# Two small loads of x and two of w1 in order of need, and tile 0's first matmuls ahead of tile 1's transposes, in a dense layer with Mish

## The chip, the cores and the metric

The kernel runs on one core of a Trainium2 chip. The metric is the device time of one execution in microseconds (us), as the median of several executions. The core has a tensor engine (PE, which multiplies matrices and transposes), a vector engine (DVE), a scalar engine (ACT, which applies functions such as Mish), GpSimd (POOL) and SyncE (SP, used here to issue transfers). Transfers run on DMA engines that SP and ACT give work to, each through a queue of its own.

## The reference

x is 2048 x 512, w1 is 512 x 1792, b1 has 1792 numbers, w2 is 1792 x 512, all bf16. The output is `mish(x @ w1 + b1) @ w2`:

```python
def reference(x, w1, b1, w2):
    h = jnp.einsum("bsd,df->bsf", x, w1) + b1
    sp = jnp.log1p(jnp.exp(-jnp.abs(h))) + jnp.where(h > 0, h, jnp.zeros_like(h))
    act = h * jnp.tanh(sp)
    return jnp.einsum("bsf,fd->bsd", act, w2)
```

## The kernel before, in words

Everything is cut into tiles of 128. The 2048 rows of x are 16 row tiles in four blocks of four. The inner size 512 has four steps k, and the hidden size 1792 has 14 tiles f. A first matmul (line 165) takes a 128 x 128 piece of w1 (k, f) as weights and streams x, transposed, past it; four of them, one for each k, add up in one PSUM bank of 512 columns. ACT reads the bank, adds the bias and writes Mish of it to `a_sb` (line 171). The second matmul (line 198) adds up 14 products of `a_sb` and w2 for each row tile; DVE copies the sum to `o_sb` (line 186) and SP stores it (line 190).

x has to be transposed. For row tiles 2 to 15 the transfer itself does that (`load_xT`, line 102). Row tiles 0 and 1 are loaded as they are into `x_nat` (line 112), one load of 256 KB in which a partition gets two neighbouring rows; PE transposes them against an identity matrix that POOL builds (`transpose_x`, line 141) and DVE copies the result from PSUM to `xT` (line 150). The output rows of tiles 0 and 1 are stored through the same pairing of rows (`out01`, line 189).

The order on each engine is written out by hand. A wait stops an engine's own queue, so what stands behind it waits as well.

- SP issues, in this order: x of tiles 0 and 1; w1 of f 0-3, k 2-3; w1 of f 4-7, k 0-1 and k 2-3; xT of tiles 2-3; w1 of f 8-13 in two; w2 in two; xT of the other blocks; later the stores.
- ACT waits for a memset of DVE (line 108), issues w1 of f 0-3, k 0-1 (line 117) and then b1 (line 118), and loads its function table (line 128).
- PE runs ten dummy matmuls on constants (line 134; five of 512 columns and five of 128, the list `WARM`), then eight transposes in three groups: k 0, k 1, and k 2-3, both row tiles in each. Then come the first matmuls of f 0-3, k by k, on the 256 columns of row tiles 0 and 1; the same for f 4-7; then f 0-7 on the 256 columns of row tiles 2 and 3, and behind each f its Mish. From f 8 on, all matmuls have 512 columns.
- DVE copies the three groups of transposes, then waits for b1 and brings it into one column for each f (lines 209 to 214), then copies outputs.

`pe.wait` in `mm1_step` (lines 161 to 164) makes a matmul wait for its bank, its piece of w1, and its columns of `xT`.

Of the kernel before, what the change touches and what calls it, by code (L numbers as in the profile page):

```python
# [4 lines left out]

P = 128
WARM = (512,) * 5 + (128,) * 5
GROUPS = ((0, 4), (4, 8), (8, 14))
BLOCKS = (512, 512, 512, 512)
LAST = 96  # L10

# [22 lines left out]
def bass_standalone__dense_activation_mish__prompt_kernel(  # L34
# [10 lines left out]
    BF, F32 = dt.bfloat16, dt.float32  # L45
# [3 lines left out]
    KT, FT = D // P, F // P  # L49
    assert (S, D, F) == (2048, 512, 1792) and sum(BLOCKS) == S  # L50
    x2, out2 = x[0], out[0]
# [3 lines left out]
    F0 = 8  # L55

    with ExitStack() as es:
        def sb(name, shape, t):
            return es.enter_context(nc.sbuf_tensor(name, shape, t))

        x_nat = sb("x_nat", [P, 2, D], BF)
        xT = sb("xT", [P, KT, S], BF)
        w1_sb = sb("w1_sb", [P, KT, F], BF)
        w2_sb = sb("w2_sb", [P, FT, D], BF)
        b1_nat = sb("b1_nat", [FT, P], BF)
# [4 lines left out]
        ident = sb("ident", [P, P], BF)  # L70
        a_sb = sb("a_sb", [P, FT, S], BF)
        o_sb = sb("o_sb", [P, S // P, D], BF)
        ps = es.enter_context(nc.psum_tensor("ps", [P, 8, 512], F32))

        def sem(name):
            return es.enter_context(nc.semaphore(name))

        sp = Stream(nc.sync, None)
        pe = Stream(nc.tensor, sem("c_pe"))
        dve = Stream(nc.vector, sem("c_dve"))  # L80
        act = Stream(nc.scalar, sem("c_act"))
        pool = Stream(nc.gpsimd, sem("c_pool"))

        def load(q, dst, src, name, transpose=False):
            s = sem(name)
            (q.eng.dma_start_transpose if transpose else q.eng.dma_start)(dst, src).then_inc(s, 16)
            return (s, 16)

        t_w1, t_w2, t_xT = {}, {}, {}

        def load_w1(q, ks, a, b):
            t = load(q, w1_sb[:, ks, a * P:b * P], w1v[:, ks, a * P:b * P], "s_w1_%d_%d" % (ks.start, a))
            for f in range(a, b):
                for k in range(ks.start, ks.stop):
                    t_w1[k, f] = t

        def load_w2(a, b):
            t = load(sp, w2_sb[:, a:b, :], w2v[:, a:b, :], "s_w2_%d" % a)
            for f in range(a, b):
                t_w2[f] = t  # L100

        def load_xT(lo, hi):
            t = load(sp, xT[:, :, lo:hi], x2[lo:hi, :], "s_xT%d" % lo, True)
            for j in range(lo // P, hi // P):
                t_xT[j] = t

        t_bz = dve.mark(nc.vector.memset(b1_pad[:, :], 0.0))  # L107
        act.wait(t_bz)

        x01 = x2[0:2 * P, :].rearrange("(p j) d -> p j d", j=2)  # L110
        out01 = out2[0:2 * P, :].rearrange("(p j) d -> p j d", j=2)
        t_xn = load(sp, x_nat[:, :, :], x01, "s_xn")
        for a, b in GROUPS:
            if a == F0:
                load_xT(2 * P, 4 * P)
            for ks in (slice(0, 2), slice(2, KT)):
                load_w1(act if (a, ks.start) == (0, 0) else sp, ks, a, b)
        t_b1 = load(act, b1_nat[:, :], b1.rearrange("(j p) -> j p", p=P), "s_b1")
        load_w2(0, 5)
        load_w2(5, FT)  # L120
        for s in range(1, len(BLOCKS)):
# [4 lines left out]
        t_id = pool.mark(pool.eng.affine_select(ident[:, :], ones[:, :], pattern=[[1, P]], compare_op=ALU.is_equal,  # L126
                                                fill=0.0, base=0, channel_multiplier=-1))
        act.eng.preload_act_table(ACT.Mish)  # L128

        c_w = nc.const_aps.tensor(1.0, [P, P], BF)  # L130
        c_m = nc.const_aps.tensor(1.0, [P, 512], BF)

        def dummy(n):
            nc.tensor.matmul(ps[:, 7, 0:n], c_w, c_m[:, 0:n], start=True, stop=True)  # L134

        free = [[] for _ in range(8)]
        t_cp = {}
        t_mish = {}


        def transpose_x(bank, ks):
            pe.wait(t_xn, t_id, *free[bank])
            psb = ps[:, bank, :].bitcast(BF)
            for i, k in enumerate(ks):
                for j in range(2):
                    mm = nc.tensor.transpose(psb[:, (2 * i + j) * P:(2 * i + j + 1) * P],  # L146
                                             x_nat[:, j, k * P:(k + 1) * P], ident[:, :])
            n = len(ks)
            dve.wait(pe.mark(mm))
            t = dve.mark(nc.vector.tensor_copy(xT[:, ks[0]:ks[0] + n, 0:2 * P],  # L150
                                               psb[:, 0:2 * n * P].rearrange("p (k t) -> p k t", k=n)))
            for k in ks:
                t_cp[k] = t
            free[bank] = [t]

        def mm1_step(s, f, k, bank, j0=0, j1=None):
            j1 = BLOCKS[s] // P if j1 is None else j1
            lo, hi = j0 * P, j1 * P
            first = k == 0 and j0 == 0
            if first:  # L160
                pe.wait(*free[bank])
            pe.wait(t_w1[k, f])
            for j in range(starts[s] // P + j0, starts[s] // P + j1):
                pe.wait(t_cp[k] if j < 2 else t_xT[j])
            return nc.tensor.matmul(ps[:, bank, lo:hi], w1_sb[:, k, f * P:(f + 1) * P],  # L165
                                    xT[:, k, starts[s] + lo:starts[s] + hi], start=first,
                                    stop=(k == KT - 1 and hi == BLOCKS[s]))
# [8 lines left out]
        s_out = sem("s_out")  # L176
        n_out = 0

        def put(i, lo, hi, bank, t_mm, q):
            nonlocal n_out  # L180
            if q is act:
                act.wait(t_mm)
                t = act.mark(act.eng.activation(o_sb[:, i, lo:hi], ps[:, bank, 0:hi - lo], ACT.Copy))  # L183
            else:
                dve.wait(t_mm)
                t = dve.mark(nc.vector.tensor_copy(o_sb[:, i, lo:hi], ps[:, bank, 0:hi - lo]))  # L186
            free[bank] = [t]
            q.wait(t)
            dst = out01[:, i, lo:hi] if i < 2 else out2[i * P:(i + 1) * P, lo:hi]
            q.eng.dma_start(dst, o_sb[:, i, lo:hi]).then_inc(s_out, 16)  # L190
            n_out += 1

        def mm2(i, lo, hi, bank, q=sp):
            s = max(b for b in range(len(BLOCKS)) if starts[b] <= i * P)
            pe.wait(*free[bank])
            for f in range(FT):
                pe.wait(t_w2[f], t_mish[s, f])
                mm = nc.tensor.matmul(ps[:, bank, 0:hi - lo], a_sb[:, f, i * P:(i + 1) * P], w2_sb[:, f, lo:hi],  # L198
                                      start=(f == 0), stop=(f == FT - 1))
            put(i, lo, hi, bank, pe.mark(mm), q)  # L200


        for n in WARM:
            dummy(n)
        transpose_x(6, (0,))
        transpose_x(5, (1,))
        transpose_x(4, (2, 3))
        dve.wait(t_b1, t_bz)
        t_b1p = dve.mark(nc.vector.tensor_copy(b1_pad[0:FT, :], b1_nat[:, :]))  # L209
        dve.wait(t_b1p)  # L210
# [1 line left out]
            t_b1t = dve.mark(nc.vector.transpose(b1_t[c * 32:(c + 1) * 32, :], b1_pad[:, c * 32:(c + 1) * 32]))  # L212
        dve.wait(t_b1t)
        t_b1c = dve.mark(nc.vector.tensor_copy(b1_sb[:, :], b1_t[:, 0:FT]))  # L214
        for a, b in GROUPS[:2]:
            for k in range(KT):
                for f in range(a, b):
                    mm1_step(0, f, k, f, 0, 2)
        for f in range(F0):
            for k in range(KT):  # L220
                mm = mm1_step(0, f, k, f, 2, 4)
            mish(0, f, f, pe.mark(mm))

        for s in range(len(BLOCKS)):
            for f in range(F0 if s == 0 else 0, FT):
                bank = f % 8 if s == 0 else 4 + f % 4
                for k in range(KT):
                    mm = mm1_step(s, f, k, bank)
                mish(s, f, bank, pe.mark(mm))
            for i in range(starts[s] // P, starts[s + 1] // P):  # L230
                if i < S // P - 1:
                    mm2(i, 0, D, i % 4)
                else:
                    mm2(i, 0, D - LAST, i % 4)
                    mm2(i, D - LAST, D, (i + 1) % 4, act)
# [29 lines left out]
```

## Time and profile before

| What | us |
|---|---|
| three runs | 105.36, 105.79, 104.87 |
| their median | 105.36 |
| the profiled execution, its own time | 105.59 |
| its span, from the first to the last instruction | 104.3 |
| PE busy | 101.6 |
| ACT busy | 38.9 |
| DVE busy | 13.2 |

The profile follows one execution. Each engine's instructions have a start and a length; PEld is the loading of weights on PE, which runs beside its matmuls. Matmuls overlap in their pipeline, so the length of one is longer than the step from one to the next. A queue row (SPq, ACTq) shows when an engine issued a transfer and how long issuing took; the rows of transfers give the time from issue to landing. Times in the rows are counted from the start of the span.

### The profile page before, as it was taken

How to read it: one execution, taken by the hardware profiler on the slowest of the kernel's cores; microseconds unless marked ns; L12 is line 12 of the kernel's file. 1: busy time of each engine (PE TensorE's matmuls, PEld its weight loads, DVE VectorE, ACT ScalarE, POOL GpSimd, SP SyncE). 2: the span in 40 equal slices, each digit the busy share in tenths (PEclk: the TensorE clock that was granted, in tenths of full speed). 3: DMA queues.
4: the chain of work that ended last, by engine and by line, in shares of the span. 5: the costliest groups of instructions: out<-in, count | busy, mean ns of one | idle time of the engine just before them, and what ended most of it. 6: DMA issues, size and time to landing. Idle time of an engine off the chain costs nothing.

```text
span 104.3 us, 1168 instructions
## 1 busy us (share of the span) xinstructions
PE 101.6 (97%) x512; PEld 50.0 (48%) x512; DVE 13.2 (13%) x26; ACT 38.9 (37%) x58; POOL 0.7 (1%) x6
## 2 busy tenths in 40 slices
PE   6999999999999999999999999999999999999992
PEld 2689744444444444444444444444444444444452
DVE  0340000022220000022220000022112000021222
ACT  1303998000027777200007777500005777700000
POOL 2000000000000000000000000000000000000000
PEclk9999999999999999999999999999999999999999
DMA  2999999981101000010111000001111000001111
GB/s 48 360 296 356 351 257 142 258 202 50 37 14 50 0 0 6 0 49 1 50 50 50 0 0 0 9 0 50 50 50 50 0 0 0 0 6 50 50 50 50
DMA packets 13377, 7.94 MB, mean 76 GB/s; under 512 B 7868, under 2 KB 13244, under 8 KB 13372
## 3 DMA queue, kind: packets, MB, share of 16 engines
q1 hardware_dynamic: 12928, 7.58, 27.6%
q10 hardware_dynamic: 444, 0.29, 0.9%
q8 instruction: 4, 0.07, 0.3%
q14 instruction: 1, 0.01, 0.0%
HBM read 3.94 MB, written 2.10 MB: 58 GB/s over the span
## 4 chain that ended last, share of the span: by engine, by line
PE 97%; ACT 0%; issue 0%
PE ps L165 47%; PE ps L198 46%; PE ps L134 3%; PE ps L146 1%; ACT o_sb L183 0%
## 5 line engine op out<-in xcount | busy, mean ns | idle before, releaser
L171 ACT ACTIVATE a_sb<-ps,b_sb 128x512 bf16<-128x512 f32 x56 | 37.4, 693 | 50.1 <-PE ps L165 50.1
L165 PE MATMUL ps<-xT,w_sb 128*128 128x512 bf16 (+1 forms) x256 | 50.0, 357 | 0.0
L198 PE MATMUL ps<-w_sb,a_sb 128*128 128x512 bf16 (+2 forms) x238 | 49.0, 366 | 0.0
L165 PEld LDWEIGHTS ps<-xT,w_sb 128*128 128x128 bf16 x256 | 25.4, 100 | 23.6
L198 PEld LDWEIGHTS ps<-w_sb,a_sb 128*128 128x128 bf16 x238 | 22.6, 98 | 26.1
L186 DVE CAST o_sb<-ps 128x512 bf16<-128x512 f32 (+1 forms) x16 | 11.0, 685 | 84.8 <-PE ps L198 84.8
L183 ACT ACTIVATE o_sb<-ps 128x96 bf16<-128x96 f32 x1 | 0.3, 251 | 11.4 <-PE ps L198 11.4
L134 PE MATMUL ps<-const-bfloat16-1.0 128*128 128x512 bf16 (+1 forms) x10 | 2.8, 469 | 0.8 <-PEq L250 0.8
L134 PEld LDWEIGHTS ps<-const-bfloat16-1.0 128*128 128x128 bf16 x10 | 1.2, 142 | 2.2 <-issue 2.2
L128 ACT ACT_TABLE_LOAD x1 | 1.3, 1283 | 2.2 <-issue 2.2
L150 DVE COPY xT<-ps 128x256 bf16<-128x256 bf16 (+1 forms) x3 | 0.9, 336 | 3.2 <-PE ps L146 3.1
L146 PE MATMUL ps<-ident,x_nat 128*128 128x128 bf16 x8 | 1.0, 311 | 0.0
L146 PEld LDWEIGHTS ps<-ident,x_nat 128*128 128x128 bf16 x8 | 0.8, 142 | 0.3 <-DMA x_nat<-in_x_dram 0.3
L212 DVE STREAM_TRANSPOSE b_t<-b_pad 32x32 bf16<-32x32 bf16 x4 | 0.8, 202 | 0.1
L126 POOL TENSOR_SCALAR_AFFINE_SELECT ident<-ones 128x128 bf16<-128x128 bf16 x1 | 0.3, 294 | 0.1
L107 DVE MEMSET b_pad<- 32x64 uint32 x1 | 0.1, 112 | 0.9 <-PEq L250 0.9
L124 POOL MEMSET ones<- 128x128 bf16 x1 | 0.2, 205 | 0.3 <-POOLq L250 0.3
L209 DVE COPY b_pad<-b_nat 14x128 bf16<-14x128 bf16 x1 | 0.2, 182 | 0.2 <-DMA b_nat<-in_b_dram 0.2
L214 DVE CAST b_sb<-b_t 128x14 f32<-128x14 bf16 x1 | 0.2, 175 | 0.0
L250 POOL MEMSET const-bfloat16-1.0<- 128x1 bf16 x1 | 0.1, 102 | 0.0
L250 POOL MEMSET const-uint8-127<- 128x1 uint8 x1 | 0.1, 102 | 0.0
L250 POOL MEMSET const-float32-0.0<- 128x1 f32 x1 | 0.1, 99 | 0.3 <-issue 0.3
(1 smaller groups left out, 0.1 us busy)
## 6 DMA issues: line engine op xcount, KB each, us to landing
out_dram<-o_sb SPq DMA_DIRECT2D x15, 128.0 KB, 1.7
w_sb<-in_w_dram SPq DMA_DIRECT2D x1, 1152.0 KB, 10.1
w_sb<-in_w_dram SPq DMA_DIRECT2D x3, 256.0 KB, 4.2
w_sb<-in_w_dram SPq DMA_DIRECT2D x2, 384.0 KB, 5.4
w_sb<-in_w_dram SPq DMA_DIRECT2D x1, 640.0 KB, 7.2
x_nat<-in_x_dram SPq DMA_DIRECT2D x1, 256.0 KB, 2.8
w_sb<-in_w_dram ACTq DMA_DIRECT2D x1, 256.0 KB, 3.4
out_dram<-o_sb SPq DMA_DIRECT2D x1, 104.0 KB, 1.7
```

The source lines that it names most:

```text
L126: t_id = pool.mark(pool.eng.affine_select(ident[:, :], ones[:, :], pattern=[[1, P]], compare_op=ALU.is_equal, fill=0.0, base=0, channel_mu ...
L128: act.eng.preload_act_table(ACT.Mish)
L134: nc.tensor.matmul(ps[:, 7, 0:n], c_w, c_m[:, 0:n], start=True, stop=True)
L146: mm = nc.tensor.transpose(psb[:, (2 * i + j) * P:(2 * i + j + 1) * P], x_nat[:, j, k * P:(k + 1) * P], ident[:, :])
L150: t = dve.mark(nc.vector.tensor_copy(xT[:, ks[0]:ks[0] + n, 0:2 * P], psb[:, 0:2 * n * P].rearrange("p (k t) -> p k t", k=n)))
L165: return nc.tensor.matmul(ps[:, bank, lo:hi], w1_sb[:, k, f * P:(f + 1) * P], xT[:, k, starts[s] + lo:starts[s] + hi], start=first, stop=( ...
L171: t = act.mark(act.eng.activation(a_sb[:, f, starts[s]:starts[s + 1]], ps[:, bank, 0:BLOCKS[s]], ACT.Mish, bias=b1_sb[:, f:f + 1]))
L183: t = act.mark(act.eng.activation(o_sb[:, i, lo:hi], ps[:, bank, 0:hi - lo], ACT.Copy))
L186: t = dve.mark(nc.vector.tensor_copy(o_sb[:, i, lo:hi], ps[:, bank, 0:hi - lo]))
L198: mm = nc.tensor.matmul(ps[:, bank, 0:hi - lo], a_sb[:, f, i * P:(i + 1) * P], w2_sb[:, f, lo:hi], start=(f == 0), stop=(f == FT - 1))
L212: t_b1t = dve.mark(nc.vector.transpose(b1_t[c * 32:(c + 1) * 32, :], b1_pad[:, c * 32:(c + 1) * 32]))
L250: nc = _bacc.Bacc("TRN2", target_bir_lowering=False, num_devices=1)
```

## The change

- `WARM` loses its five dummies of 128 columns; a list `GAP` with one dummy of 128 is run behind the transposes of row tile 0.
- x of tiles 0 and 1 is loaded in two loads of 128 KB, one for each row tile, without the pairing of rows; the stores of these tiles follow that.
- SP issues, in this order: x tile 0; w1 of f 0-3, k 0; x tile 1; w1 of f 0-3, k 1; w1 of f 0-3, k 2-3; w1 of f 4-7 in two; xT of tiles 2-3; w1 of f 8-13 in two; then as before. ACT issues none of w1.
- ACT no longer waits for DVE's memset. It loads its table, waits for x tile 0, and then issues b1.
- `transpose_x` now works on one row tile. PE transposes tile 0 (k 0, then k 1-3), runs the dummy, multiplies tile 0 by k 0 of f 0-3 (128 columns), transposes tile 1 (k 0-1, then k 2-3), multiplies tile 0 by k 1, then tile 1 by k 0 and k 1. From k 2 of f 0-3 on, both row tiles are taken together as before.

```diff
-WARM = (512,) * 5 + (128,) * 5
-GROUPS = ((0, 4), (4, 8), (8, 14))
+WARM = (512,) * 5
+GAP = (128,)
...
-        act.wait(t_bz)
-
-        x01 = x2[0:2 * P, :].rearrange("(p j) d -> p j d", j=2)
-        out01 = out2[0:2 * P, :].rearrange("(p j) d -> p j d", j=2)
-        t_xn = load(sp, x_nat[:, :, :], x01, "s_xn")
-        for a, b in GROUPS:
-            if a == F0:
-                load_xT(2 * P, 4 * P)
-            for ks in (slice(0, 2), slice(2, KT)):
-                load_w1(act if (a, ks.start) == (0, 0) else sp, ks, a, b)
-        t_b1 = load(act, b1_nat[:, :], b1.rearrange("(j p) -> j p", p=P), "s_b1")
+        def load_x(j):
+            t_xn[j] = load(sp, x_nat[:, j, :], x2[j * P:(j + 1) * P, :], "s_xn%d" % j)
+
+        load_x(0)
+        load_w1(sp, slice(0, 1), 0, 4)
+        load_x(1)
+        load_w1(sp, slice(1, 2), 0, 4)
+        load_w1(sp, slice(2, KT), 0, 4)
+        for ks in (slice(0, 2), slice(2, KT)):
+            load_w1(sp, ks, 4, F0)
+        load_xT(2 * P, 4 * P)
+        for ks in (slice(0, 2), slice(2, KT)):
+            load_w1(sp, ks, F0, FT)
         load_w2(0, 5)
...
         act.eng.preload_act_table(ACT.Mish)
+        act.wait(t_xn[0])
+        t_b1 = load(act, b1_nat[:, :], b1.rearrange("(j p) -> j p", p=P), "s_b1")
...
-        def transpose_x(bank, ks):
-            pe.wait(t_xn, t_id, *free[bank])
-            psb = ps[:, bank, :].bitcast(BF)
+        def transpose_x(j, bank, ks):
+            pe.wait(t_xn[j], t_id, *free[bank])
+            psb = ps[:, bank, 0:2 * P].bitcast(BF)
             for i, k in enumerate(ks):
-                for j in range(2):
-                    mm = nc.tensor.transpose(psb[:, (2 * i + j) * P:(2 * i + j + 1) * P],
-                                             x_nat[:, j, k * P:(k + 1) * P], ident[:, :])
+                mm = nc.tensor.transpose(psb[:, i * P:(i + 1) * P], x_nat[:, j, k * P:(k + 1) * P], ident[:, :])
...
-        transpose_x(6, (0,))
-        transpose_x(5, (1,))
-        transpose_x(4, (2, 3))
+        transpose_x(0, 6, (0,))
+        transpose_x(0, 5, (1, 2, 3))
+        for n in GAP:
+            dummy(n)
+        for k in range(2):
+            for f in range(4):
+                mm1_step(0, f, k, f, 0, 1)
+            if k == 0:
+                transpose_x(1, 6, (0, 1))
+                transpose_x(1, 4, (2, 3))
         dve.wait(t_b1, t_bz)
...
-        for a, b in GROUPS[:2]:
-            for k in range(KT):
-                for f in range(a, b):
+        for k in range(2):
+            for f in range(4):
+                mm1_step(0, f, k, f, 1, 2)
+        for a in (0, 4):
+            for k in range(0 if a else 2, KT):
+                for f in range(a, a + 4):
                     mm1_step(0, f, k, f, 0, 2)
```

More of the change, by code (lines that the diff above doesn't have):

```diff
@@ L87, in load @@
             return (s, 16)
-        t_w1, t_w2, t_xT = {}, {}, {}
+        t_xn, t_w1, t_w2, t_xT = [None] * 2, {}, {}, {}
         def load_w1(q, ks, a, b):
@@ L138, in bass_standalone__dense_activation_mish__prompt_kernel @@
         t_mish = {}
-        def transpose_x(bank, ks):
-            pe.wait(t_xn, t_id, *free[bank])
-            psb = ps[:, bank, :].bitcast(BF)
+        def transpose_x(j, bank, ks):
+            pe.wait(t_xn[j], t_id, *free[bank])
+            psb = ps[:, bank, 0:2 * P].bitcast(BF)
             for i, k in enumerate(ks):
-                for j in range(2):
-                    mm = nc.tensor.transpose(psb[:, (2 * i + j) * P:(2 * i + j + 1) * P],
-                                             x_nat[:, j, k * P:(k + 1) * P], ident[:, :])
+                mm = nc.tensor.transpose(psb[:, i * P:(i + 1) * P], x_nat[:, j, k * P:(k + 1) * P], ident[:, :])
             n = len(ks)
             dve.wait(pe.mark(mm))
-            t = dve.mark(nc.vector.tensor_copy(xT[:, ks[0]:ks[0] + n, 0:2 * P],
-                                               psb[:, 0:2 * n * P].rearrange("p (k t) -> p k t", k=n)))
+            t = dve.mark(nc.vector.tensor_copy(xT[:, ks[0]:ks[0] + n, j * P:(j + 1) * P],
+                                               psb[:, 0:n * P].rearrange("p (k t) -> p k t", k=n)))
             for k in ks:
-                t_cp[k] = t
+                t_cp[j, k] = t
             free[bank] = [t]
@@ L163, in mm1_step @@
             for j in range(starts[s] // P + j0, starts[s] // P + j1):
-                pe.wait(t_cp[k] if j < 2 else t_xT[j])
+                pe.wait(t_cp[j, k] if j < 2 else t_xT[j])
             return nc.tensor.matmul(ps[:, bank, lo:hi], w1_sb[:, k, f * P:(f + 1) * P],
@@ L188, in put @@
             q.wait(t)
-            dst = out01[:, i, lo:hi] if i < 2 else out2[i * P:(i + 1) * P, lo:hi]
-            q.eng.dma_start(dst, o_sb[:, i, lo:hi]).then_inc(s_out, 16)
+            q.eng.dma_start(out2[i * P:(i + 1) * P, lo:hi], o_sb[:, i, lo:hi]).then_inc(s_out, 16)
             n_out += 1
```

## The prediction

> **What bounds the kernel now.** I read the page first: the span, the engines' shares, and the chain of work that ended last.
>
> ```profile
> span 104.3 us, 1168 instructions
> ...
> PE 101.6 (97%) x512; PEld 50.0 (48%) x512; DVE 13.2 (13%) x26; ACT 38.9 (37%) x58; POOL 0.7 (1%) x6
> ...
> PE 97%; ACT 0%; issue 0%
> ```
>
> TensorE (PE) is busy 97% of the span and carries 97% of the chain. Then I read the same chain in order of time (start us, length us, what).
>
> ```profile
> 0.84 2.83 PE ps L134 x10
> 3.67 1.03 PE ps L146 x8
> 4.70 13.06 PE ps L165 x88
> 17.75 12.09 PE ps L198 x56
> 29.84 12.09 PE ps L165 x56
> ```
>
> From 3.67 on, PE goes from transposes to matmuls without a pause that the chain shows. A full-width matmul costs 12.09 / 56 = 0.216 us, and one of 256 columns half of it, 0.108. Is PE as quick at the start? Two stretches of equal length, line 165 alone (busy us, matmuls that touch the stretch, then clock, DMA share, GB/s):
>
> ```profile
> 4.53:6.40 1.87, 1.87 (x9) 1.00 1.15 337
> 6.40:8.27 1.87, 1.87 (x20) 1.00 1.12 297
> ```
>
> The shape is the same (256 columns, f tiles 0-7), but nine touch the first stretch and twenty the second. Nine in 1.87 is 0.208 each, twice 0.108. The granted-clock column says 1.00 in both rows, so it hides this; the counts show PE at half rate until about 6.40. **Everything the diff moves on PE lies in this slow stretch, so 1 us saved there brings only 0.5 us at the end**, unless the turn at 6.40 moves as well. That is the question of this case.
>
> The weight loads say what PE waits for at the start, and the same pair of rows prices small dummies.
>
> ```profile
> 2.50 0.15 PEld L134 LDWEIGHTS ps<-const-bfloat16-1.0 128*128 128x128 bf16 x1 [0.28 <-issue]
> 2.93 0.47 PEld L134 LDWEIGHTS ps<-const-bfloat16-1.0 128*128 128x128 bf16 x4 [0.28 <-issue]
> 3.66 0.77 PEld L146 LDWEIGHTS ps<-ident,x_nat 128*128 128x128 bf16 x8 [0.26 <-DMA x_nat<-in_x_dram]
> ```
>
> A 512-column dummy holds PE 2.93 - 2.50 = 0.43 us. Four 128-column loads in 0.47 are three steps of 0.107 and one load of 0.15; so a 128-column step is 0.107 us here. PE then stands 0.26 us until x has landed, and the first transpose starts at 3.66.
>
> **The loads.** The queue rows, then issue to landing of the first ones (KB, us):
>
> ```profile
> 0.81 0.39 SPq L86 DMA_DIRECT2D x_nat<-in_x_dram  x1
> 1.26 1.44 SPq L86 DMA_DIRECT2D w_sb<-in_w_dram  x3
> 2.74 1.30 SPq L86 DMA_TRANSPOSE xT<-in_x_dram  x1
> ```
>
> ```profile
> x_nat<-in_x_dram SPq DMA_DIRECT2D x1, 256.0 KB, 2.8
> w_sb<-in_w_dram ACTq DMA_DIRECT2D x1, 256.0 KB, 3.4
> ```
>
> ```profile
> w_sb<-in_w_dram SPq DMA_DIRECT2D x1, 256.0 KB, 3.9
> ```
>
> ```profile
> xT<-in_x_dram SPq DMA_TRANSPOSE x1, 5.0
> ```
>
> ScalarE's queue and its part of the start:
>
> ```profile
> 1.02 0.43 ACTq L86 DMA_DIRECT2D w_sb<-in_w_dram  x1
> 1.47 0.72 ACTq L86 DMA_DIRECT2D b_nat<-in_b_dram  x1
> 2.22 1.28 ACT L128 ACT_TABLE_LOAD   x1 [2.22 <-issue]
> 9.62 3.00 ACT L171 ACTIVATE a_sb<-ps,b_sb 128x512 bf16<-128x512 f32 x5 [6.12 <-PE ps L165]
> ```
>
> So x lands at 0.81 + 2.8 = 3.6, w1 k 0-1 of f 0-3 at 1.02 + 3.4 = 4.4, k 2-3 at 1.26 + 3.9 = 5.2, xT of tiles 2-3 at 2.74 + 5.0 = 7.7. One 256 KB load follows another by 0.74 to 0.8 us: in order, at full DMA. How fast the bytes come in (last column GB/s):
>
> ```profile
> 1.80:2.40 0.60, 0.60 (x3) 0.15 (x1) 0.00 (x0) 0.18 (x1) 0.00 (x0) 1.00 0.99 126
> 2.40:2.90 0.50, 0.50 (x2) 0.15 (x1) 0.00 (x0) 0.50 (x1) 0.00 (x0) 1.00 0.85 301
> 2.93:3.66 0.73, 0.73 (x6) 0.47 (x5) 0.00 (x0) 0.58 (x1) 0.00 (x0) 1.00 1.03 356
> ```
>
> **Part 1: x in two loads, w1 k 0 and k 1 between and behind.** Tile 0 is 128 KB (131 kB) where 256 KB stood. At those rates 76 kB are in by 2.40 and 131 kB by 2.58; the whole 262 kB were in by 3.00. The gain lies between 0 (the landing is latency, not bytes) and 0.42. I take 0.30, nearer the upper end, since later landings follow the bytes. So x tile 0 lands at 3.31 and its first transpose starts at 3.36. After it each 128 KB costs 0.37, half of 0.74: w1 k 0 at 3.68, x tile 1 at 4.05, k 1 at 4.42, k 2-3 at 5.2, the same bytes as now by the same time. SP issues all of it, one per 0.48 (1.44 / 3): the five issues start at 0.81, 1.26, 1.74, 2.22, 2.70, and with 2.5 from issue to landing no load can beat 4.24 (x tile 1), 4.72 (k 1) and 5.20 (k 2-3). I use these later values.
>
> **Part 2: the order on PE.** DVE's rows give the way from a transpose to a matmul.
>
> ```profile
> 4.09 1.06 DVE L150 COPY xT<-ps 128x256 bf16<-128x256 bf16 x3 [3.11 <-PE ps L146]
> 5.33 0.18 DVE L209 COPY b_pad<-b_nat 14x128 bf16<-14x128 bf16 x1 [0.17 <-DMA b_nat<-in_b_dram]
> 5.54 0.90 DVE L212 STREAM_TRANSPOSE b_t<-b_pad 32x32 bf16<-32x32 bf16 x4
> 6.48 0.17 DVE L214 CAST b_sb<-b_t 128x14 f32<-128x14 bf16 x1
> ```
>
> ```profile
> L150 DVE COPY xT<-ps 128x256 bf16<-128x256 bf16 x2 | 0.5, 292 | 3.1 <-PE ps L146 3.1
> L150 DVE COPY xT<-ps 128x512 bf16<-128x512 bf16 x1 | 0.4, 423 | 0.1
> ```
>
> Two transposes from 3.66 release the copy at 4.09, 0.43 later; one does so after 0.32. A copy of 128 columns isn't in the trace. The line through 292 ns (256) and 423 ns (512) gives 227 for 128 and 161 for none, so it lies between 0.16 and 0.29; I take 0.23. From a copy's end (4.09 + 0.29 = 4.38) to the first matmul (4.53) are at most 0.15, part of it the weights' wait; I take 0.13. All in slow-stretch time:
>
> - 3.36 first transpose of tile 0; four and the GAP dummy, 5 x 0.107, end at 3.90.
> - Copy of k 0: 3.36 + 0.32 = 3.68 to 3.91; first matmul at 4.04. **A stall of 0.14 that is not there now.** w1 k 0 (3.68, or 1.26 + 2.5 = 3.76) is not what it waits for.
> - Four matmuls of 128 columns to 4.47; tile 1's four transposes (x landed 4.24) to 4.90; k 1 of tile 0 (weights 4.72; its copy of three blocks is done by about 4.5) to 5.32.
> - Tile 1's copy of k 0-1: 4.47 + 0.43 + 0.29 + 0.13 = 5.32: just in time. Eight matmuls of 128 to 6.18.
>
> Sixteen matmuls of 128 columns are eight of 256. The kernel before does its eight from 4.53 in 8 x 0.208, to 6.20. So the sum at that point is -0.30 (x sooner) + 0.107 (GAP) + 0.14 (stall) + 0.03 (handing over, rounding) = **-0.02 us, worth -0.01 us at the end.** The five small dummies cost nothing either way: they stand in the wait for x, which lasts from 2.93 to 3.36 without them; an x before 2.93 would be needed for them to matter. With the bounds (gain 0 to 0.42, copy 0.07 faster to 0.06 slower) the sum is -0.21 to +0.34, worth -0.11 to +0.17.
>
> **Part 3: later loads.** xT of tiles 2-3 is issued eighth on SP rather than fifth, at about 4.2 (0.81 + 7 x 0.48) instead of 2.74. The bytes ahead of it are the same 1280 KB, so by bytes it lands at 7.7 again; with its own 5.0 from issue it would be 9.2. PE needs it after 32 matmuls: 9 to 6.40 and 23 x 0.108 give 8.9. I take 7.8, free, since most of the 5.0 was queueing behind loads that are now gone before it is issued; at 9.2 it costs 0.3 at full rate. w1 of f 8-13 and w2 keep their place in bytes behind it.
>
> b1 is issued by ScalarE once x tile 0 is in, 3.31 rather than 1.47. From its issue to DVE's use were 5.33 - 1.47 = 3.86; then the chain to 6.65, 1.32. That gives 8.5; the first Mish starts at 9.62, released by PE. Cover 1.1; and DVE holds no transpose copy behind that wait. The table load moves to about 1 on ScalarE, which has nothing before 9.62. Output rows of tiles 0 and 1 change place in DRAM, not size: nothing, as the end comes from later tiles.
>
> **The rivals.** *PE's turn to full rate comes later (slower).* Today PE starts at 0.84, stands 0.26 once, and turns at 6.40, 5.56 after its start. The changed kernel stands from 2.93 (2.50 + 0.43) to 3.36 and again 0.14: 0.57, twice as much and earlier. If the standing makes the clock's count begin anew at 3.36, the turn comes at 8.92, 2.52 late, at half rate **+1.26: 106.6**. It decides once the standing is too much; that 0.26 was not is all the trace says. The Trainium skill ("TensorE: Matmul & The Clock Gate", Part 1) gives free-running windows of about 3.4 us, of which one must be busy; by it a missed window would cost an estimated 1.7 us rather than 1.26. Its Part 4 says of transposes that they don't count as busy in the same way; by that rule the 0.85 us of transposes would add to both kernels' standing, making this rival likelier. The trace has one turn and can't show either. Against it: eight transposes and a wait stood ahead of the turn now too. Chance 0.18.
>
> *The change doesn't do what it says*: tile 0 lands with tile 1, as the queue's start is what takes the time (the 126 GB/s row). Then PE starts at 3.66 as now, and the GAP and the stall remain: +0.28 slow, +0.14; with xT late (+0.3) **105.6 to 105.8**. Chance 0.14.
>
> *The gain comes whole and more*: x tile 0 at 3.1 or below (0.5 sooner), w1 k 0 right behind, no second stall: -0.5 + 0.25 slow, **105.2**. For: the last quarter of the load came at 301 to 356 GB/s. Chance 0.13. *The turn comes sooner*, by 2 us or more, for a reason not in the rows (other executions differ by 0.9 us): **104.3**, chance 0.05.
>
> **How the numbers follow.** The profiled execution took 105.59, with 104.3 span; the median of the runs is 105.36, 0.23 lower, and they reach from 104.87 to 105.79. 105.59 - 0.01 - 0.23 is 105.35; I say 105.3. Chances: forecast (within 0.2 of now) 0.50, rivals as above. Low end: the early case and the runs' spread, 104.8; high end: up to the late turn, 106.5, leaving half of that rival out. About 1% (1.05 us) is what a measurement of this kernel can tell from no change. Faster by over 1% is the sooner turn: 0.05. Slower by over 1% is the late turn, whose 1.26 the spread may hide: 0.17. Same: 0.78.
>
> **What would show it.** First transposes between 3.2 and 3.5 (x split right); a gap of about 0.14 ahead of the first matmul, released by DVE's copy (the stall); 128-column steps of 0.107; two half-length stretches around 6.40 with about nine and twenty matmuls' worth of columns (turn unmoved); no PE wait at about 8.9 (xT in time). It is wrong if the half-rate stretch ends at 8 or later, if PE waits for x tile 1 or w1 by more than 0.2, or if Mish waits for the bias.

## The result

The changed kernel takes 105.94 us (median of 19 executions, 105.64 to 107.56) against 105.27 for the kernel before (19 executions, 104.66 to 105.85). The ratio is 1.0069, with a 95% interval of 1.0049 to 1.0089: slower by 0.7%, where no change was forecast. Here and below a median is over all executions, while a ratio leaves out those more than 1.5% above the fastest of their kernel, here the one of 107.56. The ranges matter as much as the medians. Before, times spread evenly over 1.2 us; afterwards the fastest execution stands 1 us above the fastest before, and most lie within 0.5 us of each other. The change put a floor under the time.

The chain of waits of the changed kernel shows the floor (start us, length us, what):

```profile
2.66 3.63 DMA w_sb<-in_w_dram
6.30 0.05 issue
6.34 11.47 PE ps L167 x80
17.81 12.09 PE ps L199 x56
29.90 12.09 PE ps L167 x56
```

Before, PE alone carried the chain. Now a load of w1 stands in it for 3.63 us: the fifth load on SP, w1's k 2-3 of f 0-3, issued at 2.66 and landed at 6.30. In the kernel before it landed at 5.2. From 6.34 on PE runs without a pause that the chain shows.

The weight loads of the changed kernel, in order of time, show how PE came there (in brackets how long they stood idle just before, and what the profile says ended it):

```profile
2.94 0.35 PEld L149 LDWEIGHTS ps<-ident,x_nat 128*128 128x128 bf16 x4 [0.72 <-DMA x_nat<-in_x_dram]
3.25 0.15 PEld L138 LDWEIGHTS ps<-const-bfloat16-1.0 128*128 128x128 bf16 x1
3.62 0.24 PEld L167 LDWEIGHTS ps<-xT,w_sb 128*128 128x128 bf16 x4 [0.22 <-DMA w_sb<-in_w_dram]
4.06 0.23 PEld L149 LDWEIGHTS ps<-ident,x_nat 128*128 128x128 bf16 x4 [0.20 <-DMA x_nat<-in_x_dram]
4.55 0.67 PEld L167 LDWEIGHTS ps<-xT,w_sb 128*128 128x128 bf16 x12 [0.27 <-DMA w_sb<-in_w_dram]
6.34 0.66 PEld L167 LDWEIGHTS ps<-xT,w_sb 128*128 128x128 bf16 x7 [1.11 <-DMA w_sb<-in_w_dram]
```

The start is early: first transpose at 2.94 (3.66 before). Then PE waits three times for copies and loads, 0.20 to 0.27 us each, and at last its weight loads stand 1.11 us for k 2-3 of w1. Four weight loads took 0.35 at 2.94 and 0.24 at 3.62, and twelve took 0.67 at 4.55, which is 0.056 a step where the prediction read 0.107 at half rate. So PE is at full rate here by about 3.62, whereas the profiled execution of the kernel before turned at 6.40. **The two profiled executions (105.64 and 105.59) are therefore not like with like.** The later traces show this turn at other times again. The changed kernel's trace has an early turn and still ends as late as the other kernel's late one.

The bytes show that the load came late because the transfers were slow. Three stretches of the kernel before, then of the changed one (last column GB/s):

```profile
2.90:3.90 1.00, 1.00 (x9) 0.71 (x8) 0.00 (x0) 0.61 (x1) 0.00 (x0) 1.00 1.02 350
3.90:4.90 1.00, 1.00 (x10) 0.82 (x8) 0.67 (x3) 0.00 (x0) 0.00 (x0) 1.00 1.07 367
4.90:5.90 1.00, 1.00 (x7) 0.74 (x5) 0.77 (x4) 0.00 (x0) 0.00 (x0) 1.00 1.08 359
```

```profile
2.90:3.90 1.00, 1.00 (x10) 0.69 (x9) 0.53 (x2) 0.00 (x0) 0.00 (x0) 1.00 0.82 236
3.90:4.90 1.00, 0.87 (x13) 0.57 (x11) 0.54 (x3) 0.00 (x0) 0.00 (x0) 1.00 0.79 161
4.90:5.90 1.00, 0.50 (x9) 0.33 (x6) 0.00 (x0) 0.00 (x0) 0.00 (x0) 1.00 0.96 290
```

The transfers move 350 to 367 GB/s before, and 161 to 290 after. Over these three microseconds that is 0.39 MB less, more than the 256 KB that PE then waits for.

The traces also hold each packet. In these three microseconds the median packet took 0.046 us in both kernels. But 14 packets of the changed kernel, 1 KB each, took more than 0.3 us, up to 0.78; in the kernel before it was one, of 0.33. So the stream is held up by a few packets that take long, and not only by engines that have nothing to do: in the stretch of 161 GB/s they were busy for 0.79 of the time.

### The profile page after: what moved, and what is told of

Read it like the earlier page. It is cut to its first block, busy times and chain, and to the rows that moved or that the text cites. A ratio compares the mean times of both kernels' runs of the same rounds, so it can differ in the third digit from the quotient of the medians.

```text
span 104.4 us, 1180 instructions
## 1 busy us (share of the span) xinstructions
PE 100.5 (96%) x516; PEld 48.9 (47%) x516; DVE 13.3 (13%) x27; ACT 38.9 (37%) x58; POOL 0.7 (1%) x6
## 4 chain that ended last, share of the span: by engine, by line
PE 92%; DMA 3%; SPq 2%; issue 0%; ACT 0%
PE ps L199 46%; PE ps L167 46%; DMA w_sb<-in_w_dram 3%; SPq L86 2%; ACT o_sb L185 0%
## 5 line engine op out<-in xcount | busy, mean ns | idle before, releaser
L167 PE MATMUL ps<-xT,w_sb 128*128 128x512 bf16 (+2 forms) x264 | 49.4, 347 | 1.0 <-DMA w_sb<-in_w_dram 0.9
L138 PEld LDWEIGHTS ps<-const-bfloat16-1.0 128*128 128x128 bf16 x6 | 0.7, 133 | 1.6 <-issue 1.6
L152 DVE COPY xT<-ps 128x256 bf16<-128x256 bf16 (+2 forms) x4 | 1.1, 289 | 2.8 <-PE ps L149 2.7
```

The lines of the kernel that those rows point to most:

```text
L152: t = dve.mark(nc.vector.tensor_copy(xT[:, ks[0]:ks[0] + n, j * P:(j + 1) * P], psb[:, 0:n * P].rearrange("p (k t) -> p k t", k=n)))
```

## The experiments

Each ratio is against the kernel before on the same chip, with its 95% interval. "Landing" is that of w1's k 2-3 of f 0-3 in the profiled execution: its issue plus its issue-to-landing time. There is one trace of each kernel, and the two of the changed kernel differ by 0.45 us in this landing. The change itself measured 1.0069 above and 1.0115 in its second run, so differences of a few tenths of a per cent between two variants are not resolved.

**The changed kernel again**, for a second trace (no edit).

> The changed kernel once more, for a second trace. Theory A (the queue): w1 of k 2-3 for f 0-3, issued fifth at 2.7 us, always lands late, at 6.0 to 6.5 us, and PE waits for it at the 256-column matmuls; the time is 105.9 whatever the clock does. Theory B (the clock): the trace fell on one early turn of PE's clock, and another execution with the turn at 6 us or later shows no wait for w1; the time then comes from the standing of PE. Theory C (an accident of one execution): w1 lands at 5.2 and nothing waits.

Measured: 106.43 us, ratio 1.0115 (1.0072 to 1.0158). Its chain of waits and its matmuls of the first layer in two equal stretches:

```profile
2.66 4.08 DMA w_sb<-in_w_dram
6.75 0.05 issue
6.79 4.88 PE ps L167 x28
```

```profile
6.80:10.18 3.38, 3.38 (x16) 1.00 1.15 264
10.18:13.56 3.38, 3.38 (x32) 1.00 1.08 350
```

The load lands at 6.75, and PE waits for it again: no accident. This profiled execution took 107.73 us, more than the others, because PE turned to full rate only at 10.2 us (16 matmuls, then 32). So theory A holds for the load. The late turn of theory B exists as well, but the five other executions, 106.00 to 106.54, are not like this one.

**b1 early:**

```diff
-        act.wait(t_xn[0])
-        t_b1 = load(act, b1_nat[:, :], ...)
+        t_b1 = load(act, b1_nat[:, :], ...)      # first thing on ScalarE's queue
```

> The changed kernel with b1 issued by ScalarE at once, as before, rather than behind x tile 0. Rival D: b1's small packets, which now move between 4.3 and 5.5 us beside w1's k 2-3, are what slows that load; then it lands at 5.2 to 5.4 and the time falls to 105.3 or below. Theory A: the load still lands at 6 or later and the time stays at 105.8 to 106.0.

Measured: 106.02 us, ratio 1.0091 (1.0063 to 1.0118); landing at 6.5. So b1's late place is not the cause of the late load.

**Loads alone, and order alone.** The first takes the changed loads with the order on PE of before (`pe.wait(*t_xn, ...)` ahead of all transposes), the second the reverse (one load of x, w1's first on ScalarE's queue).

> The changed loads under the order on PE of before (all eight transposes behind both tiles of x, ten dummies, 256-column matmuls throughout). Theory A: w1's k 2-3 lands at 6.0 or later here too, PE waits for it, and the time is 105.9 or more. Rival E (the order on PE and its 128-column matmuls cost the time): no more than 105.3 plus 0.2 for x tile 1 at 4.0.

> The loads of before (x in one, w1's first on ScalarE's queue, b1 early) under the changed order on PE, with the ten dummies of before. Theory A: w1's k 2-3 lands at 5.2 and the time is 105.3 to 105.4, by the dummy and the stall of 0.14 at half rate. Rival E: the time is 105.9.

Measured: loads alone 106.23 us, ratio 1.0118 (1.0071 to 1.0166), landing at 7.0. Order alone 105.44, ratio 1.0030 (1.0002 to 1.0058), landing at 1.26 + 3.8 = 5.1. The loads carry the loss; the order costs about 0.3 us by itself, and the two don't add up. The loss of the loads alone isn't all the one landing's, though: in that trace the first transposes start at 4.36, behind x tile 1, and the chain doesn't pass through k 2-3. The weight loads in the trace with the order alone show where its 0.3 us may go:

```profile
4.41 0.23 PEld L162 LDWEIGHTS ps<-xT,w_sb 128*128 128x128 bf16 x4 [0.41 <-DMA w_sb<-in_w_dram]
4.59 0.27 PEld L144 LDWEIGHTS ps<-ident,x_nat 128*128 128x128 bf16 x4
4.82 0.27 PEld L162 LDWEIGHTS ps<-xT,w_sb 128*128 128x128 bf16 x4
5.30 0.17 PEld L162 LDWEIGHTS ps<-xT,w_sb 128*128 128x128 bf16 x3 [0.22 <-DVE xT L147]
```

Here PE turned early, so four matmuls take 0.23, and tile 1's transposes are over before DVE has copied them: PE waits 0.22 for the copy. The prediction found this place "just in time" at half rate. At full rate it is not. The first row shows a second place: the matmuls wait 0.41 for w1, and tile 1's transposes, for which x had been there since 0.81 + 2.7 = 3.5, stand behind them. In the kernel before these transposes fill that time. No run separates the two.

**Which property of the loads?** Four kernels change one or two of them. `two_rings` lets ScalarE issue k 0 and k 1; `merged_w1` makes them one load on SP; `one_ring` and `w1_quarters` start from the kernel before:

```diff
two_rings (from the changed kernel)
-        load_w1(sp, slice(0, 1), 0, 4)
+        load_w1(act, slice(0, 1), 0, 4)
-        load_w1(sp, slice(1, 2), 0, 4)
+        load_w1(act, slice(1, 2), 0, 4)
merged_w1 (from the changed kernel)
-        load_w1(sp, slice(0, 1), 0, 4)
+        load_w1(sp, slice(0, 2), 0, 4)
-        load_w1(sp, slice(1, 2), 0, 4)
one_ring (from the kernel before)
-                load_w1(act if (a, ks.start) == (0, 0) else sp, ks, a, b)
+                load_w1(sp, ks, a, b)
w1_quarters: as one_ring, and f 0-3 in four loads, one for each k
```

> The changed kernel with w1's k 0 and k 1 of f 0-3 issued by ScalarE (b1 behind them as in the change), so that the same five loads are issued in half the time. Theory A1 (SP issues one load per 0.47 us, 128 KB moves in 0.37, so the queue runs dry between loads and starts anew each time): w1's k 2-3 lands at 5.0 to 5.4, the wait of about 1 us is gone, and the time is 105.0 to 105.3. Rival A2 (loads of 128 KB are slow by themselves, whoever issues them): it lands at 6 or later and the time stays at 105.9.

> The changed kernel with w1's k 0-1 of f 0-3 in one load of 256 KB between the two loads of x, all on SP: four issues rather than five for the same bytes. Theory A1: the 256 KB piece gives the queue a stock, w1's k 2-3 lands at 5.0 to 5.4; the time is 105.1 to 105.4. Rival A3 (one ring for everything is slow): it lands at 6 or later, 105.9.

> The kernel before with its first w1 load moved from ScalarE's queue to SP's, behind x: everything on one ring, in pieces of 256 KB. Theory A1: no dry queue, since 256 KB takes 0.74 us to move and 0.47 to issue; w1's k 2-3 lands at 5.2 and the time is as before, 105.1. Rival A3 (one ring): later than 5.8, and slower by 0.3 or more.

> The kernel before with all loads on SP, x whole, and w1 of f 0-3 in four loads of 128 KB, one for each k. Theory A1: x's 256 KB come first and are slow to start, so the four are issued before they are needed; k 3 lands at 5.2 to 5.5 and the time is within 0.2 of before. Rival A2 (128 KB loads are slow by themselves): k 3 lands at 6 or later, and the time is 105.7 or more.

| Kernel | median us | ratio (interval) | landing us |
|---|---|---|---|
| two_rings | 105.88 | 1.0065 (1.0036 to 1.0094) | 6.5 |
| merged_w1 | 106.13 | 1.0105 (1.0071 to 1.0139) | 6.2 |
| one_ring | 105.76 | 1.0054 (1.0021 to 1.0087) | 5.9 |
| w1_quarters | 105.48 | 1.0037 (1.0008 to 1.0066) | 5.8 (k 3) |

Theory A1, a queue that runs dry because SP issues too slowly, falls: in `two_rings` k 2-3 was issued at 1.72, 0.94 sooner than in the changed kernel, and landed at 6.5, between that kernel's 6.30 and 6.75; in `merged_w1` it landed at 6.2 where A1 said 5.0 to 5.4. Loads of 128 KB are not the whole of it either, since `one_ring` has none and is slow; `w1_quarters` fits neither theory. **Moving one 256 KB load from ScalarE's queue to SP's, with no other edit, costs 0.5%.** The move also puts the issue of k 2-3 back, from 1.26 to 1.72. That alone doesn't make it late: in `x_split` below it is issued at 1.72 too, and lands 3.6 later, at 5.3. The chain of `one_ring`, and the row of `x_split`:

```profile
1.72 4.15 DMA w_sb<-in_w_dram
```

```profile
w_sb<-in_w_dram SPq DMA_DIRECT2D x1, 256.0 KB, 3.6
```

In `one_ring` the slow stretch is short and late; the rate falls to 263 GB/s:

```profile
2.90:3.90 1.00, 0.89 (x8) 0.60 (x7) 0.00 (x0) 0.06 (x1) 0.00 (x0) 1.00 1.05 371
3.90:4.90 1.00, 0.86 (x11) 0.69 (x10) 0.72 (x3) 0.00 (x0) 0.00 (x0) 1.00 0.98 263
4.90:5.90 1.00, 0.75 (x7) 0.43 (x5) 0.87 (x6) 0.00 (x0) 0.00 (x0) 1.00 0.92 285
```

**x split, with w1's first load back on ScalarE's queue; and two attempts at a cause.**

```diff
x_split (from the changed kernel)
+        act.wait(t_bz)
         load_x(0)
-        load_w1(sp, slice(0, 1), 0, 4)
         load_x(1)
-        load_w1(sp, slice(1, 2), 0, 4)
+        load_w1(act, slice(0, 2), 0, 4)
+        t_b1 = load(act, b1_nat[:, :], ...)      # and not behind x tile 0
touch_w1, touch_w2 (from the changed kernel)
+        touch = sb("touch", [P, KT, 32], BF)
...
+        load(act, touch[:, :, :], w1v[:, :, F0 * P:F0 * P + 32], "s_touch")   # or w2v[:, 10:14, 0:32]
         load_x(0)
```

> The changed kernel with w1's k 0-1 of f 0-3 back in one load of 256 KB on ScalarE's queue, and b1 behind it, as before; x stays in two loads on SP, and the order on PE is the changed one. Theory F (what hurts is that w1's first part left ScalarE's queue): w1's k 2-3 lands at 5.0 to 5.4 as in the run with the order alone, nothing waits 0.5 us for it, and with x tile 0 at about 2.9 the time is 105.0 to 105.3, at or under the 105.4 of the order alone. Rival G (x in two loads of 1 KB rows disturbs the loads behind it): it lands at 5.8 or later and the time is 105.7 or more.

> The changed kernel with one more small load on ScalarE's queue at the start: 64 bytes of each of w1's 512 rows (32 KB in all, from columns that nothing else reads early) into a tile that nobody uses. Rival H (the first access of a DMA engine to a region of DRAM is slow, 0.4 to 1 us, and each load of w1 meets it afresh): the long packets at 3 to 5 us go, w1's k 2-3 lands by 5.5, and the time falls below 105.5. Theory F: no change beyond 0.2 us, since the early part of w1 still shares SP's ring.

> As the run that touches w1, but the small load reads 64 bytes of each of 512 rows of w2. Rival H: no gain, as w1's rows are still untouched: 105.9 and w1's k 2-3 at 6 or later. If both small loads help alike, it is a second stream at the start that helps and not the touching.

`x_split`: 105.45 us, ratio 1.0026 (0.9998 to 1.0055), landing at 1.72 + 3.6 = 5.3. That is the time of the order alone, where theory F said 105.0 to 105.3. So its landing holds, x in two loads does not delay k 2-3, and rival G falls. No gain shows either, and the weight loads say why:

```profile
3.00 0.35 PEld L148 LDWEIGHTS ps<-ident,x_nat 128*128 128x128 bf16 x4 [0.78 <-DMA x_nat<-in_x_dram]
3.30 0.15 PEld L137 LDWEIGHTS ps<-const-bfloat16-1.0 128*128 128x128 bf16 x1
4.21 0.23 PEld L166 LDWEIGHTS ps<-xT,w_sb 128*128 128x128 bf16 x4 [0.76 <-DMA w_sb<-in_w_dram]
```

The transposes start at 3.00, and then PE waits 0.76 us for w1. `touch_w1` (1.0113, 1.0063 to 1.0163; landing 5.9) and `touch_w2` (1.0152, 1.0093 to 1.0210; landing 6.5) don't help, and their traces still have 11 and 10 packets over 0.3 us from 2.9 to 5.9 us. Three of `touch_w2`'s six executions took 107.20 to 107.41, which raises its ratio. So a small early read of these rows, in by 0.80 + 2.4 = 3.2, cures nothing, and rival H finds no support; that some other first access is slow isn't excluded.

**The price of the landing by itself, and what ScalarE's load must be like.** `late_k23` moves one load of the kernel before; the other two start from `x_split`.

```diff
late_k23 (from the kernel before; xT and f 8-13 follow as they did)
+        load_w1(act, slice(0, 2), 0, 4)
+        load_w1(sp, slice(0, 2), 4, F0)
+        load_w1(sp, slice(2, KT), 4, F0)
+        load_w1(sp, slice(2, KT), 0, 4)
x_split_halves
-        load_w1(act, slice(0, 2), 0, 4)
+        load_w1(act, slice(0, 1), 0, 4)
+        load_w1(act, slice(1, 2), 0, 4)
x_split_b1late: b1 again behind x tile 0
```

> The kernel before, with nothing changed but the place of one load: w1's k 2-3 of f 0-3 goes behind the two loads of f 4-7 on SP, so that it lands at 6.5 to 6.8 rather than 5.2, as late as in the changed kernel, with the same bytes in all. If this load's landing is what the change lost by, PE waits for it, the 256-column matmuls of k 2 start at 6.6 to 6.9, and the time is 105.7 to 106.1, 0.5 to 1.0 above before. If the landing doesn't matter, the time stays within 0.2 of before.

> The run with x split and w1's k 0-1 on ScalarE's queue, with these two k as two loads of 128 KB there. Theory F1 (any early stream of w1 on ScalarE's queue keeps the loads quick): k 2-3 lands at 5.0 to 5.4, k 0 lands at 3.6 to 3.8 rather than 4.2, so PE's first matmuls come sooner, and the time is 105.2 to 105.4. Rival F2 (it has to be one load of 256 KB; halves run slow wherever they are, as in the run with two rings): k 2-3 lands at 6 or later, 105.8 or more.

> The run with x split and w1's k 0-1 on ScalarE's queue, but b1 as late as in the changed kernel, behind x tile 0. If b1's late issue counts once w1 is on ScalarE's queue (the run with two rings had it late and was slow), k 2-3 lands at 5.8 or later and the time is 105.8. If not, it lands at 5.0 to 5.4 and the time is 105.4.

`late_k23`: 106.08 us, ratio 1.0097 (1.0059 to 1.0135). Its chain:

```profile
2.23 4.63 DMA w_sb<-in_w_dram
6.86 0.05 issue
6.90 3.24 PE ps L167 x28
```

With the loads otherwise quick and PE's order of before, one late landing alone costs about 1 us (0.6 to 1.4) and makes the floor: five of its six executions lie between 105.98 and 106.24. That is the changed kernel's picture, at a landing 0.56 later, and it shows that a landing as late as this is enough for the whole loss.

`x_split_halves`: 106.01 us, ratio 1.0051 (1.0022 to 1.0081); k 1 landed at 1.42 + 4.5 = 5.9, k 2-3 at 1.72 + 4.9 = 6.6. `x_split_b1late`: 105.52 us, ratio 1.0019 (0.9988 to 1.0050), landing at 5.3. So b1's place moves neither the median nor this landing, and two halves on ScalarE's queue don't do what the one 256 KB load does. (In the trace of `x_split_b1late` the next load of w1 landed at 7.0, though, and PE waited 0.51 for it; `x_split` had it at 6.1.)

What remains open is why. Every kernel with one 256 KB load of w1 early on ScalarE's queue and k 2-3 next to be loaded of w1 on SP has it at 5.1 to 5.3 (the kernel before, the order alone, `x_split`, `x_split_b1late`); every kernel without such a load has it at 5.8 to 7.0. The long packets go with this: from 2.9 to 5.9 us the quick kernels (with `late_k23`, whose other loads are quick) have 1 to 6 packets over 0.3 us, all others 9 to 19. No run tells what in the queues or in DRAM makes these packets long.

Nor is k 2-3 always the load that PE waits for last. The chain passes through it in both traces of the changed kernel, `b1_early`, `one_ring` and `late_k23`; through a load of f 4-7 in `merged_w1`, `touch_w1` and `x_split_b1late`; through k 1 in `touch_w2` and `x_split_halves`; through x tile 0 in `two_rings`; through k 0-1 in the order alone and `x_split`, where the stream is quick; and through no load in the loads alone and in `w1_quarters`. In the variants a late k 2-3 is the sign of a slow stream, and the loss need not be its own.

## Why the prediction was wrong

**The step that failed** is the landing of w1's k 2-3: "k 2-3 at 5.2, the same bytes as now by the same time". It took the rate of the kernel before, one 256 KB load per 0.74 us, for a property of the bytes. The runs show that it depends on how they are queued. The new set of loads ran at 161 to 290 GB/s where 350 to 367 had been, and the load landed at 6.30 (6.75 in the second trace). The prediction named "if PE waits for x tile 1 or w1 by more than 0.2" as what would make it wrong; its weight loads waited 1.11. It gave this no rival with a chance, though, and the bound it used for k 2-3, 5.20 from issue, was a lower one alone. Nor did "no load can beat" hold: x tile 1 landed at 1.72 + 2.3 = 4.0 and k 1 at 2.19 + 2.3 = 4.5, before 4.24 and 4.72. That 105.94 lies within the stated 104.8 to 106.5 is luck: the high end stood for a late turn of PE, not for a late load.

**x tile 0** came sooner than forecast: 2.1 us from issue, at 2.9, so 0.7 earlier rather than 0.30 within "0 to 0.42". The upper bound was wrong, as it took the first 0.6 us of slow bytes (126 GB/s) for granted; with the smaller load that stretch (1.80 to 2.40) moved 215 GB/s. Its landing and the stretch:

```profile
x_nat<-in_x_dram SPq DMA_DIRECT2D x1, 128.0 KB, 2.1
```

```profile
1.80:2.40 0.60, 0.60 (x3) 0.15 (x1) 0.00 (x0) 0.28 (x1) 0.00 (x0) 1.00 0.89 215
```

This gain was lost later, in the wait for k 2-3.

**The order on PE.** A copy of 128 columns took 225 ns (0.23 forecast). DVE's part of the start in the changed kernel, and the copy's row among its groups:

```profile
3.28 0.68 DVE L152 COPY xT<-ps 128x128 bf16<-128x128 bf16 x2 [2.29 <-PE ps L149]
4.38 0.49 DVE L152 COPY xT<-ps 128x256 bf16<-128x256 bf16 x2 [0.43 <-PE ps L149]
6.08 0.18 DVE L217 COPY b_pad<-b_nat 14x128 bf16<-14x128 bf16 x1 [1.21 <-DMA b_nat<-in_b_dram]
6.30 0.90 DVE L220 STREAM_TRANSPOSE b_t<-b_pad 32x32 bf16<-32x32 bf16 x4
7.23 0.17 DVE L222 CAST b_sb<-b_t 128x14 f32<-128x14 bf16 x1
```

```profile
L152 DVE COPY xT<-ps 128x128 bf16<-128x128 bf16 x1 | 0.2, 225 | 2.3 <-PE ps L149 2.3
```

The dummy and the wait for DVE were there: the GAP's load of weights starts at 3.25, the first matmul's at 3.62, and the profile puts its 0.22 down to a DMA, though w1's k 0 had landed at 3.4; the copy ended last, at 3.28 + 0.225 = 3.50. So the stall came where it was forecast, at 0.22 for 0.14. By the prediction's own terms the order costs 0.107 + 0.14 + 0.03 at half rate, some 0.14 us at the end. The order alone measured 0.3% (0.02 to 0.58%), which doesn't contradict that; that such a wait counts in full where the turn comes early may be why it is more, but no run shows it.

**"1 us saved there brings only 0.5 us at the end"** held for one execution, not for the kernel. The turn at 6.40 was read as the kernel's; other traces have it by 3.62 (the changed kernel) and at 10.2 (the same kernel again). The Trainium skill ("TensorE: Matmul & The Clock Gate", Part 1) says that the turn varies between runs, as its windows are free-running; these three traces agree with that, and the prediction used it for one rival alone.

**The rivals.** The late turn that the prediction priced at +1.26, with a chance of 0.18, did come in single executions: the one of 107.73 turned at 10.2, and of the changed kernel's 25 executions one more, without a trace, took as long (107.56). None of the 117 executions of the kernel before, over all these runs, took more than 106.11. So a changed start seems to make it possible, though no run shows by what; it moved `touch_w2`'s median (its trace, of 107.20, has 15 matmuls from 7.10 to 9.20 and 22 in the next 2.10 us), and not the changed kernel's.

xT of tiles 2-3 landed at 4.17 + 4.7 = 8.9, inside the bounds 7.7 to 9.2 and 1.1 later than taken. It caused no wait, but only just: PE, itself held up, came to it at about 6.34 + 24 x 0.108 = 8.9. b1 was in place at 7.40 (7.23 + 0.17 in DVE's rows above) where 8.5 was taken, and the Mish didn't wait for it, as forecast.

## What to carry to other kernels

A transfer rate read from a trace belongs to that set of queues and sizes; a change that regroups the loads needs a rival in which the last of them is late, with its price. When a load that comes first is made to come sooner, ask for the ones that PE needs after it: the landing that it waits for last sets the floor. And before a start-up stretch is costed, find out whether its length is the same in each execution: where it isn't, one trace of each kernel can make a loss of 0.7% look like a tie.

## What the runs showed that was not expected

Which queue carries a load changed the landing of other loads. `one_ring` differs from the kernel before in one queue name and costs 0.54% (0.21 to 0.87%), with k 2-3 at 5.9 rather than 5.2. The Trainium skill ("DMA: Bandwidth & Descriptors", Rules for kernel authors) says that spreading loads over SP and ScalarE doesn't help bandwidth and only saves time to issue; here the rate after the start differed, 263 against 367 GB/s in the same microsecond of one trace each, and the measurement decides.

The granted-clock column said 1.00 in each stretch shown here, also in those at half rate (16 matmuls against 32 in equal time). In the first 10 us of these kernels the steps between matmuls tell the rate; that column doesn't.
